# A fused top-k attention and feed-forward kernel: the first pair loaded in parts, and identity products ahead of it

## The chip, the cores and the metric

The kernel runs on one core of a Trainium2 chip. The time is device microseconds of one execution. The kernel before was run six times; the time quoted for it is the median, 874.3 us. One further execution was recorded by the hardware profiler, and every duration below comes from it.

## The reference

For 8 batches and 8 heads, with 576 positions and a head dimension of 64, each row of attention scores keeps its 32 largest entries. The softmax runs over those alone. The heads are laid side by side to rows of 512, and these go through a feed-forward with a squared ReLU.

```python
scores = scale * np.matmul(q, k.transpose(0, 1, 3, 2))
kth = np.partition(scores, -top_k, axis=-1)[..., -top_k:-top_k + 1]
mask = scores >= kth
scores = np.where(mask, scores, -1000000000.0)
...
attn = attn / (np.sum(attn, axis=-1, keepdims=True) + 1e-09)
return np.matmul(attn, v).astype(np.float32)
...
h = x @ w_in
r = np.maximum(h, 0.0)
g = r * r
return (g @ w_out).astype(np.float32)
```

The inputs are float32: q, k and v of 8 x 8 x 576 x 64, w_in of 512 x 2048, w_out of 2048 x 512. The output is 4608 x 512.

## The kernel before

**Tiles.** Two heads make a pair, and there are 32 pairs. The 576 query rows of a pair make four groups of 128 rows (gi 0 to 3) and a rest of 64 rows; the rests of two pairs make one more group (gi is Z). That gives 144 groups, each with 128 query rows of two heads on the partitions. The feed-forward works on chunks of up to 256 rows as soon as all heads of those rows are done.

**What one pair and one group go through.**

- `load_pair` loads q, k and v of a pair (tiles rq, rk, rv; two buffers each). q and k take three DMAs each (L469 twice, L472), v takes five (L479, L483). TensorE transposes q and k in blocks of 128 rows against a float32 identity (through the helper at L447): four blocks of q, four of k, and two short blocks of 64 rows. ScalarE copies the results from PSUM to the tile qk (L511 to L514). POOL converts v to bf16 (L515).
- `top_k` makes the scores of one group: eight float32 products into three PSUM banks (helper at L444). There is one such set of banks, so the next group's scores wait until the present ones are read. ScalarE copies them to s (L555). VectorE reads PSUM and s for pairwise maxima (L611, twice), which are merged once more (L621). POOL makes the matching minima from sums on the int32 patterns (L606). Then VectorE takes eight maxima at a time (L638), replaces them (L642), three times for each head, and takes the last eight over all 576 (L645), whose last one is the 32nd largest.
- ScalarE marks what is below it (w, L653). `attend` transposes the scores back with that mask added (L447, L444), ScalarE takes the exponential (p, L687), and `collect` multiplies with v and scales by the reciprocal of the sum (L714 to L742, the reciprocal on VectorE, L716).
- `feed` does the feed-forward of a chunk: products with win, ReLU (L768), square (L779 on VectorE for the last chunk, L782 on POOL), products with wo, copy (L802), store.
- `setup` makes the identities on POOL and loads and converts the sixteen weight parts (L891, L894). Their staging lies in two buffers.

PSUM has eight banks: three for the scores, two for `attend` together with one more (ps_q, which the merge shares), and two (the pool `psum`) for every transposition of q and k and every product of `collect` and `feed`.

**What sets the order.** Every operation is recorded in a plan with an engine, an assumed duration, a priority (the smaller the earlier), the tiles that it reads and writes, and the buffers that it takes. `schedule` plays this plan: each time an engine is free it starts the ready operation of the smallest priority whose buffers are free. The order so found on each engine is fixed and written out. On the chip each engine runs its list in order, and waits on semaphores for what the list needs. The assumed durations thus give the order; they don't give the time. A store or load on the SP list is assumed to hold SP for 0.6 per DMA, and to end 2.3 after that. `nbf` is the earliest assumed time of an operation, and `after` and `order` name operations that must come before. A load with `via="act"` is planned in SP's list, but issued at the start by ScalarE; k of the first pair is such a load.

The priorities of a group are built from its due time `tg = T0 + PER * n`, with n the number of the group, and constants at L320 to L340:

- ME and MQ set how early VectorE merges the maxima of a group (L611 and L621), in the same unit as PER.
- TW sets when its mask is made (L653).
- TA sets when `attend` is due; for the last NL groups, TL pulls it forward, by an amount that grows linearly to the end.
- WC sets the priority of the weight conversions, WN the earliest assumed time of their loads.
- LAGL delays the products of the feed-forward of the last batch.

Of the kernel before, what the change touches and what calls it, by code (L numbers as in the profile page):

```python
# [12 lines left out]
P = 128  # L13
# [278 lines left out]
def bass_top_k_attn__then__act_relu_squared_kernel(  # L292
# [27 lines left out]
    PER = 5.55  # L320
    T0 = 12.0
    LEAD = 40
    ME = 16.41
    MQ = 15.52
    MP = 18.0
    MA = 18.98
    SQ = 5.15
    TA = 7.2
    TW = -0.14
    TL = 8.0  # L330
    NL = 28.07
    WD = 3.33
    WC = 1.75
    WA = 1.13
    WN = 6
    NBO = 3.81
    LAG = 11.28
    STEP = 3.19
    LATE = 2.38
    LAGL = 11.07  # L340

    ident32 = sb("ident32", [P, P])
    ident_bf = sb("ident_bf", [P, P], BF16)
# [102 lines left out]
    def tr(o, i, ident, **kw):  # L446
        return pe.matmul(o, i, ident, is_transpose=True, skip_group_check=True, **kw)  # L447
# [3 lines left out]
    def build(full, weights, pl):  # L451
# [3 lines left out]
        def slot_sem(o):  # L455
            t = o.takes[0]
            return f"{t.pool.name}{t.slot}"

        def load_pair(b, hp, base):
            rq, rk, rv = tile("rq"), tile("rk"), tile("rv")  # L460


            def load(t, src, rest, queue=nc.sync):
                def fn():
                    r = at(t)
                    res = []
                    for h in range(2):
                        r0 = 64 if h and rest != (512, 512) else 0
                        res.append(queue.dma_start(r[:, 0:4, h, :], src[b, 2 * hp + h, r0:r0 + 512, :].rearrange(  # L469
                            "(tb p) d -> p tb d", p=P)))  # L470
                    x = src[b, 2 * hp, rest[0]:rest[0] + 64, :]
                    res.append(queue.dma_start(r[0:64, 4, :, :], bass.AP(  # L472
                        x.tensor, x.offset, [x.ap[0], [(S + rest[1] - rest[0]) * D, 2], x.ap[1]])))
# [12 lines left out]
            pl.op("sp", 2.3, base - 80, load(rq, q, (512, 512)), w=[rq], take=[rq], sem=slot_sem, ndma=3)  # L486
            via = "act" if not full and not state["pairs"] else None
            state["pairs"] += 1
            pl.op("sp", 2.3, base - 79.9, load(rk, k, REST, nc.scalar if via else nc.sync), w=[rk], take=[rk], sem=slot_sem,
                  ndma=3, via=via)  # L490
            pl.op("sp", 2.3, base - 70, loadv, w=[rv], take=[rv], sem=slot_sem, ndma=5)
            qk, vb = tile("qk"), tile("vb")
            tq, tk, tx = Tile(psum), Tile(psum), Tile(psum)
# [18 lines left out]
            pl.op("act", .6, base - 42.4, lambda: act.copy(at(qk)[:, 640:1152], bank(tk)), r=[tk], w=[qk])  # L512
            pl.op("act", .3, base - 42.3, lambda: act.copy(at(qk)[:, 512:640], bank(tx)[:, 0:128]), r=[tx], w=[qk])
            pl.op("act", .25, base - 42.2, lambda: act.copy(at(qk)[:, 1152:1216], bank(tx)[:, 64:128]), r=[tx], w=[qk])  # L514
# [311 lines left out]
        for b in range(NB):  # L826
            seq, stages = batch_order(b)
            pairs, held = {}, {}
            last = b == NB - 1
            for hp, gi in seq:  # L830
                tg = T0 + PER * state["n"]
                hps = (hp, hp if gi != Z else hp + 1)
                for x in hps:
                    if x not in pairs:
                        pairs[x] = load_pair(b, x, tg)
                st, wt = top_k(gi, [pairs[x][0] for x in hps], tg)
                tt = tg + PER + 2 - TA - TL * max(0, 1 - (NGRP - state["n"]) / NL)
# [12 lines left out]
                if left[i] == 0:  # L850
                    tm = T0 + PER * state["n"] + (NBO if not last else 8)
                    c = CHUNKS[i]
                    feed(c, xts[i], tm, (STEP if b < NB - 2 else 1.9) if not last else (1.5 if c is not CHUNKS[-1] else .5))
        return kths, rzs

    def setup(pl):
# [22 lines left out]
        for i in range(16):  # L879
# [121 lines left out]
```

## Time and profile before

| What | Value |
|---|---|
| Median of six runs | 874.3 us |
| The six runs | 875.54, 874.66, 868.26, 873.94, 869.92, 874.95 us |
| The profiled execution: its time | 868.97 us |
| The profiled execution: its span | 867.2 us |
| TensorE busy (matmul) | 803.4 us, 93% |
| VectorE busy | 822.4 us, 95% |
| ScalarE busy | 759.8 us, 88% |
| POOL busy | 788.0 us, 91% |
| Chain that ended last, by engine | DVE 64%, PE 16%, ACT 9% |
| First VectorE instruction starts | 12.55 us |
| Last selection on VectorE (L645) starts | 837.53 us |

The span runs from the first recorded event to the last one; the execution's own time is 1.8 us longer. In the profile PE is TensorE's matrix unit, PEld its loading of the stationary operand, DVE is VectorE, ACT is ScalarE, POOL is GpSimd, and SPq is the list from which SyncE issues DMAs. A line of a timeline has the start in us, the duration in us, the engine, the line of the kernel, the operation, the tiles written and read, the shapes, and how many instructions were merged; the bracket at its end gives the idle time ahead of it and who ended it. A line of a stretch has its bounds and length, and then for each engine the busy time and the number of instructions, the granted TensorE clock, the share of the DMA engines, and GB/s. A line of the waits has the waiting engine and line, who was waited for, the sum in us, how often, and the longest. In the slices, each digit is the busy share of a fortieth of the span, in tenths.

### The profile page before, as it was taken

How to read it: one execution, taken by the hardware profiler on the slowest of the kernel's cores; microseconds unless marked ns; L12 is line 12 of the kernel's file. 1: busy time of each engine (PE TensorE's matmuls, PEld its weight loads, DVE VectorE, ACT ScalarE, POOL GpSimd, SP SyncE). 2: the span in 40 equal slices, each digit the busy share in tenths (PEclk: the TensorE clock that was granted, in tenths of full speed). 3: DMA queues.
4: the chain of work that ended last, by engine and by line, in shares of the span. 5: the costliest groups of instructions: out<-in, count | busy, mean ns of one | idle time of the engine just before them, and what ended most of it. 6: DMA issues, size and time to landing. Idle time of an engine off the chain costs nothing.

```text
span 867.2 us, 22447 instructions
## 1 busy us (share of the span) xinstructions
PE 803.4 (93%) x7911; PEld 607.7 (70%) x7970; DVE 822.4 (95%) x3413; ACT 759.8 (88%) x1261; POOL 788.0 (91%) x826
## 2 busy tenths in 40 slices
PE   4577999989999999998999999999999999999996
PEld 3455777767687777766777677777777767677784
DVE  2989999999999999999999999999999999999971
ACT  4877998989898898989989899889999889898973
POOL 6989999999999998999999889998999987999971
PEclk9999999999999999999999999999999999999999
DMA  7982212130210223012131022202221021100000
GB/s 178 227 213 60 45 41 57 28 95 17 55 43 14 67 56 80 18 40 56 29 89 25 25 65 58 71 14 55 46 67 42 14 52 44 41 2 14 26 22 33
DMA packets 126969, 48.21 MB, mean 56 GB/s; under 512 B 119168, under 2 KB 119168, under 8 KB 126848
## 3 DMA queue, kind: packets, MB, share of 16 engines
q1 hardware_dynamic: 125648, 46.39, 21.4%
q8 instruction: 65, 1.06, 0.5%
q14 instruction: 56, 0.46, 0.2%
q10 hardware_dynamic: 1200, 0.30, 0.2%
HBM read 37.22 MB, written 9.44 MB: 54 GB/s over the span
## 4 chain that ended last, share of the span: by engine, by line
DVE 64%; PE 16%; ACT 9%; issue 5%; DMA 2%; POOL 2%; SPq 2%; DVEq 0%
DVE f L642 21%; DVE c L638 16%; DVE kth L645 13%; PE ps L444 12%; DVE f L621 5%; DVE ps L611 5%; DVE m L611 4%; PE ps L447 4%; ACT s L555 2%; ACT p L687 2%; ACT w L653 1%; DMA rk<-in_k_dram 1%; ACT g L768 1%; POOL f L606 1%; POOL t L606 1%
## 5 line engine op out<-in xcount | busy, mean ns | idle before, releaser
L642 DVE MATCH_REPLACE8 f<-c,f 128x104 f32<-128x104 f32 (+2 forms) x864 | 267.2, 315 | 0.0
L638 DVE MAX8 c<-f 128x8 f32<-128x104 f32 (+2 forms) x864 | 244.0, 319 | 0.0
L447 PE MATMUL ps<-ident,s 128*128 128x128 f32 x1296 | 221.8, 280 | 21.9 <-ACT p L687 14.1
L653 ACT ACTIVATE w<-s,kth 128x576 bf16<-128x576 f32 x288 | 222.8, 786 | 19.9 <-DVE kth L645 18.7
L444 PE MATMUL ps<-qk 64*128 64x64 f32 (+3 forms) x1280 | 211.0, 449 | 8.1 <-DVE m L611 6.7
L606 POOL TENSOR_TENSOR t<-s 128x576 int32<-128x576 int32 x144 | 202.4, 1411 | 12.7 <-ACT s L555 12.6
L645 DVE MAX8 kth<-f 128x8 f32<-128x576 f32 x288 | 207.5, 747 | 0.0
L606 POOL TENSOR_TENSOR f<-t,m 128x576 int32<-128x576 int32 x144 | 203.1, 1411 | 0.1
L555 ACT COPY s<-ps 128x1152 f32<-128x1152 f32 x144 | 161.4, 1121 | 31.6 <-PE ps L444 30.6
L444 PEld LDWEIGHTS ps<-qk 64*128 64x128 f32 (+1 forms) x1280 | 130.5, 178 | 83.4 <-issue 61.9
L447 PEld LDWEIGHTS ps<-ident,s 128*128 128x128 f32 x1296 | 143.4, 141 | 48.1 <-ACT p L687 22.9
L687 ACT ACTIVATE p<-ps 128x1152 bf16<-128x1152 f32 x144 | 163.3, 1134 | 8.8 <-PE ps L444 8.0
L444 PE MATMUL ps<-steep_bf,w 128*128 128x128 bf16 x1296 | 140.8, 219 | 0.0
L444 PE MATMUL ps<-wo,g 128*128 128x512 bf16 x517 | 127.9, 379 | 4.0 <-issue 1.1
L606 POOL TENSOR_TENSOR t<-m 128x288 int32<-128x288 int32 x144 | 114.8, 797 | 17.2 <-ACT m L619 13.7
L444 PE MATMUL ps<-xt,win 128*128 128x256 bf16 (+1 forms) x1152 | 126.6, 261 | 1.5 <-ACT qk L511 0.8
L606 POOL TENSOR_TENSOR f<-t,f 128x288 int32<-128x288 int32 x144 | 114.8, 797 | 0.0
L444 PEld LDWEIGHTS ps<-xt,win 128*128 128x128 bf16 x1152 | 97.9, 98 | 15.9 <-ACT g L768 1.2
L444 PEld LDWEIGHTS ps<-steep_bf,w 128*128 128x128 bf16 x1296 | 105.7, 100 | 4.1
L782 POOL TENSOR_TENSOR g<-g 128x512 bf16<-128x512 bf16 x92 | 95.5, 1040 | 12.9 <-ACT g L768 11.7
L768 ACT ACTIVATE g<-ps 128x512 bf16<-128x512 f32 x144 | 86.0, 606 | 10.2 <-PE ps L444 9.3
L444 PEld LDWEIGHTS ps<-wo,g 128*128 128x128 bf16 x576 | 51.3, 98 | 47.9 <-ACT xt L742 0.6
(60 smaller groups left out, 879.2 us busy)
## 6 DMA issues: line engine op xcount, KB each, us to landing
rq<-in_q_dram SPq DMA_DIRECT2D x64, 128.0 KB, 2.5
rv<-in_v_dram SPq DMA_DIRECT2D x64, 128.0 KB, 2.4
out_dram<-o SPq DMA_DIRECT2D x32, 256.0 KB, 2.1
rk<-in_k_dram SPq DMA_DIRECT2D x62, 128.0 KB, 2.6
g<-in_moe_w_in_dram SPq DMA_DIRECT2D x8, 512.0 KB, 4.5
g<-in_moe_w_out_dram SPq DMA_DIRECT2D x8, 512.0 KB, 4.8
rv<-in_v_dram SPq DMA_DIRECT2D x96, 16.0 KB, 2.2
rq<-in_q_dram SPq DMA_DIRECT2D x32, 32.0 KB, 2.8
```

The costliest lines, as they stand in the source:

```text
L444: return pe.matmul(o, l, r, start=start, stop=stop, skip_group_check=True)
L447: return pe.matmul(o, i, ident, is_transpose=True, skip_group_check=True, **kw)
L555: cp = [pl.op("act", 1.2, tg - LEAD + 1, lambda: act.copy(at(st)[:, :, :], two(banks(ss), SECOND, S)), r=[ss], w=[st])]
L606: return pl.op("gp", dur, prio, lambda: gp.tensor_tensor(o().bitcast(I32), x().bitcast(I32), y().bitcast(I32), op), **kw)
L611: return vec.tensor_tensor(o, two(banks(ss)[:, a:], SECOND + HALF, QUART), two(at(st)[:, 0, HALF + a:], HALF, QUART), ALU.max)
L638: lambda i=i, t=t, c0=c0, c1=c1: vec.max(eighth(t, i), at(f)[:, i, c0:c1]),
L642: lambda i=i, t=t, c0=c0, c1=c1: vec.match_replace(at(f)[:, i, c0:c1], eighth(t, i), at(f)[:, i, c0:c1], NEG), hold=[f])]
L645: ks.append(chain(kth, i, prev[i] + [low], .665, lambda i=i: vec.max(eighth(kth, i), at(f)[:, i, :]), hold=[f]))
L653: pl.op("act", .77, tw + .8 * i, lambda i=i: act.activation(at(wt)[:, i, :], at(st)[:, i, :], ACTF.Relu, bias=kth[:, i, n:n + 1], scale=-1.0),
L687: pl.op("act", 1.15, tt + 1, lambda: act.activation(at(pt)[:, :, :].rearrange("p k q -> p (k q)"), banks(e)[:, 0:2 * S], ACTF.Exp, scale=0 ...
L768: return act.activation(at(g)[:, 0:kf * nt], bank(hh)[:, 0:kf * nt], ACTF.Relu)
L782: pl.op("gp", .15 + w_ / 480, tf + lag + 1, lambda g=g: gp.tensor_tensor(at(g)[:, 0:w_], at(g)[:, 0:w_], at(g)[:, 0:w_], ALU.mult), u=[g])
```

## The change

Four things are changed.

- **The loads of the first pair.** k is loaded first in the plan, still issued by ScalarE. q comes in two tiles: its first 128 rows of both heads (two DMAs), and then the rest (three DMAs) into the second rq buffer. Other pairs are loaded as before.
- **The transpositions of the first pair.** The first block of q, then the four full blocks of k, then the short block of k are transposed. VectorE copies the four blocks of k from PSUM; ScalarE copies the block of q, and the short block of k twice (to both ends of k's part of qk). The first group's scores are planned next. The other blocks of q, their copy, and the conversion of v are recorded after the first group's selection, by `later`.
- **Identity products.** Thirty-six products of the bf16 identity with itself repeated four times (512 columns) are planned for TensorE at the lowest priority. Each takes one bank of the pool `psum`, may start once the identity is made, and has an earliest assumed time 0.22 after the one before it. Nothing reads their results. With WEND equal to WARM, the second list of times is empty.
- **Constants.** Ten constants are changed or new.

```diff
-    ME = 16.41
-    MQ = 15.52
+    ME = 20.33
+    MQ = 19.99
...
-    TW = -0.14
-    TL = 8.0
-    NL = 28.07
+    TW = -1.88
+    TL = 12.76
+    WARM = 8
+    WSTEP = 1.2
+    WEND = 8
+    NL = 36.74
...
-    WC = 1.75
+    WC = 2.52
...
-    LAGL = 11.07
+    LAGL = 12.15
...
+            pl.op("sp", 2.3, base - 82, start(nc.scalar, lambda: part(rk, k, 0, 0, 4), lambda: part(rk, k, 1, 0, 4),
+                                           lambda: rest(rk, k, REST[0], REST[1] - REST[0])),
+                  w=[rk], take=[rk], sem=slot_sem, ndma=3, via="act")
+            pl.op("sp", 2.3, base - 81, start(nc.sync, lambda: part(rq, q, 0, 0, 1), lambda: part(rq, q, 1, 0, 1)),
+                  w=[rq], take=[rq], sem=slot_sem, ndma=2)
+            pl.op("sp", 2.3, base - 79, start(
+                nc.sync, lambda: part(rq2, q, 0, 1, 3), lambda: part(rq2, q, 1, 1, 3), lambda: rest(rq2, q, 512, 0)),
+                w=[rq2], take=[rq2], sem=slot_sem, ndma=3)
...
+            o_x = pl.op("pe", .15, base - 45.2, flips(tx, rq, [0]), r=[rq], w=[tx], take=[tx, qk])
+            o_k = pl.op("pe", .5, base - 45.1, flips(tk, rk, [0, 1, 2, 3]), r=[rk], w=[tk], take=[tk], order=[o_x])
+            pl.op("pe", .2, base - 45, lambda: tr(bank(tx)[:, 128:192], at(rk)[0:64, 4, :, :].rearrange("p h d -> p (h d)"),
+                                                  ident32[0:64, 0:64]), r=[rk], w=[tx], order=[o_k])
+            pl.op("act", .3, base - 42.5, lambda: act.copy(at(qk)[:, 0:128], bank(tx)[:, 0:128]), r=[tx], w=[qk])
+            pl.op("dve", .6, base - 42.5, lambda: vec.tensor_copy(at(qk)[:, 640:1152], bank(tk)), r=[tk], w=[qk])
+            for i, c in enumerate((576, 1152)):
+                pl.op("act", .25, base - 42.4 + .1 * i, lambda c=c: act.copy(
+                    at(qk)[:, c:c + 64], bank(tx)[:, 128:192]), r=[tx], w=[qk])
+
+            def later():
+                pl.op("pe", .5, base - 44, flips(tq, rq2, [1, 2, 3, 4]), r=[rq2], w=[tq], take=[tq])
+                pl.op("act", .6, base - 42, lambda: act.copy(at(qk)[:, 128:576], bank(tq)[:, 0:448]), r=[tq], w=[qk])
+                pl.op("gp", .8, base + 5, lambda: gp.tensor_copy(at(vb)[:, :, 0:D], at(rv)[:, :, :]),
+                      r=[rv], w=[vb], take=[vb])
+
+            state["more"] = later
+            return qk, vb
...
                 st, wt = top_k(gi, [pairs[x][0] for x in hps], tg)
+                if state.get("more"):
+                    state.pop("more")()
...
+        times = [.22 * i for i in range(int(WARM / .22))]
+        times += [WARM + WSTEP * i for i in range(int((WEND - WARM) / WSTEP))]
+        for x in times:
+            t = Tile(psum)
+            pl.op("pe", .22, 1e5, lambda t=t: mm(bank(t), ident_bf[:, :], ident_bf[:, :].unsqueeze(1).broadcast_to(
+                [P, 4, P]), True), w=[t], take=[t], after=[i2], nbf=x)
```

More of the change, by code (lines that the diff above doesn't have):

```diff
@@ L457, in slot_sem, with load_first, part, rest @@
             return f"{t.pool.name}{t.slot}"
+        def load_first(b, hp, rq, rq2, rk, base):
+            def part(t, src, h, tb, n_):
+                r0 = 128 * tb + (64 if h and src is k else 0)
+                return at(t)[:, tb:tb + n_, h, :], src[b, 2 * hp + h, r0:r0 + 128 * n_, :].rearrange(
+                    "(tb p) d -> p tb d", p=P)
+            def rest(t, src, r0, d0):
+                x = src[b, 2 * hp, r0:r0 + 64, :]
+                return at(t)[0:64, 4, :, :], bass.AP(x.tensor, x.offset, [x.ap[0], [(S + d0) * D, 2], x.ap[1]])
+            def start(queue, *parts):
+                return lambda: [queue.dma_start(*x()) for x in parts]
+            pl.op("sp", 2.3, base - 82, start(nc.scalar, lambda: part(rk, k, 0, 0, 4), lambda: part(rk, k, 1, 0, 4),
[6 more added lines that the diff above has]
+                w=[rq2], take=[rq2], sem=slot_sem, ndma=3)
@@ new lines, in first_pair, with flips, fn @@
+        def first_pair(rq, rq2, rk, rv, qk, vb, base):
+            tk, tx, tq = Tile(psum), Tile(psum), Tile(psum)
+            def flips(o, src, tbs):
+                def fn():
+                    for i, tb in enumerate(tbs):
+                        n_ = 64 if tb == 4 else 128
+                        ins = tr(bank(o)[:, 128 * i:128 * i + n_], at(src)[0:n_, tb, :, :].rearrange("p h d -> p (h d)"),
+                                 ident32[0:n_, 0:n_])
+                    return ins
+                return fn
+            o_x = pl.op("pe", .15, base - 45.2, flips(tx, rq, [0]), r=[rq], w=[tx], take=[tx, qk])
[14 more added lines that the diff above has]
+            return qk, vb
@@ L459, in load_pair, with load @@
         def load_pair(b, hp, base):
             rq, rk, rv = tile("rq"), tile("rk"), tile("rv")
-            def load(t, src, rest, queue=nc.sync):
+            def load(t, src, rest):
                 def fn():
@@ L468, in fn @@
                         r0 = 64 if h and rest != (512, 512) else 0
-                        res.append(queue.dma_start(r[:, 0:4, h, :], src[b, 2 * hp + h, r0:r0 + 512, :].rearrange(
+                        res.append(nc.sync.dma_start(r[:, 0:4, h, :], src[b, 2 * hp + h, r0:r0 + 512, :].rearrange(
                             "(tb p) d -> p tb d", p=P)))
                     x = src[b, 2 * hp, rest[0]:rest[0] + 64, :]
-                    res.append(queue.dma_start(r[0:64, 4, :, :], bass.AP(
+                    res.append(nc.sync.dma_start(r[0:64, 4, :, :], bass.AP(
                         x.tensor, x.offset, [x.ap[0], [(S + rest[1] - rest[0]) * D, 2], x.ap[1]])))
@@ L484, in loadv @@
                 return res
-            pl.op("sp", 2.3, base - 80, load(rq, q, (512, 512)), w=[rq], take=[rq], sem=slot_sem, ndma=3)
-            via = "act" if not full and not state["pairs"] else None
+            via = not full and not state["pairs"]
             state["pairs"] += 1
-            pl.op("sp", 2.3, base - 79.9, load(rk, k, REST, nc.scalar if via else nc.sync), w=[rk], take=[rk], sem=slot_sem,
-                  ndma=3, via=via)
+            if via:
+                rq2 = tile("rq")
+                load_first(b, hp, rq, rq2, rk, base)
+            else:
+                pl.op("sp", 2.3, base - 80, load(rq, q, (512, 512)), w=[rq], take=[rq], sem=slot_sem, ndma=3)
+                pl.op("sp", 2.3, base - 79.9, load(rk, k, REST), w=[rk], take=[rk], sem=slot_sem, ndma=3)
             pl.op("sp", 2.3, base - 70, loadv, w=[rv], take=[rv], sem=slot_sem, ndma=5)
             qk, vb = tile("qk"), tile("vb")
+            if via:
+                return first_pair(rq, rq2, rk, rv, qk, vb, base)
             tq, tk, tx = Tile(psum), Tile(psum), Tile(psum)
```

## Prediction

> **What bounds the kernel now.** I read the busy shares first, then the slices, then who VectorE waited for, then the first 20 us instruction by instruction, and last the end.
>
> ```profile
> PE 803.4 (93%) x7911; PEld 607.7 (70%) x7970; DVE 822.4 (95%) x3413; ACT 759.8 (88%) x1261; POOL 788.0 (91%) x826
> ...
> PE   4577999989999999998999999999999999999996
> ...
> DVE  2989999999999999999999999999999999999971
> ```
>
> VectorE is busy 95%, and the slices say where the rest is: at both ends. Cut into stretches, VectorE is busy 50.0 of every 50 us from 100 to 750. So a saving counts if it starts VectorE earlier, fills its holes before 100 us, or shortens what follows its last selection. All of VectorE's waits over 3 us:
>
> ```profile
> DVE ps L611 <- ACT s L555: 15.3, 2, 12.5
> DVE rzall L716 <- ACT av L714: 7.7, 3, 4.4
> DVE g L779 <- ACT g L768: 6.3, 4, 4.9
> DVE ps L611 <- ACT p L687: 3.7, 4, 2.0
> ```
>
> The first line is the start: 12.5 us before the first score copy, and 2.72 before the second. The second and third are the end. The fourth belongs to the holes at 41.8, 50.0 and 74.3 (0.17, 2.04 and 1.15 us). The start as a timeline:
>
> ```profile
> 5.95 1.09 PE L447 MATMUL ps<-ident,rq 128*128 128x128 f32 x4 [5.95 <-DMA rq<-in_q_dram]
> ...
> 7.92 0.58 ACT L512 COPY qk<-ps 128x512 f32<-128x512 f32 x1 [0.27 <-PE ps L447]
> ...
> 8.85 2.50 PE L444 MATMUL ps<-qk 64*128 64x64 f32 x8 [0.56 <-ACT qk L514]
> ...
> 11.40 1.12 ACT L555 COPY s<-ps 128x1152 f32<-128x1152 f32 x1 [2.60 <-PE ps L444]
> ...
> 12.55 0.47 DVE L611 TENSOR_TENSOR ps<-ps,s 128x288 f32<-128x288 f32 x1 [12.55 <-ACT s L555]
> ...
> 13.43 2.50 PE L444 MATMUL ps<-qk 64*128 64x64 f32 x8 [2.08 <-DVE m L611]
> ...
> 18.45 1.35 PE L444 MATMUL ps<-qk 64*128 64x64 f32 x8 [0.48 <-DVE f L642]
> ```
>
> The same eight score products take 2.50 us twice, then 1.35: TensorE runs at half speed until about 17.0 (four transpositions fall from 1.09 to 0.66). The clock column shows only recorded changes and reads 1.00 there; later it shows what closes the clock. Stretches of 3.4 us, with PE's busy time as the first pair of numbers:
>
> ```profile
> 40.90:44.30 3.40, 1.38 (x14) 1.26 (x16) 3.23 (x17) 3.40 (x6) 3.16 (x5) 1.00 1.04 238
> 44.30:47.70 3.40, 3.40 (x29) 2.55 (x30) 3.40 (x14) 1.13 (x3) 3.40 (x4) 0.50 0.73 180
> ...
> 13.60:17.00 3.40, 3.40 (x14) 2.56 (x15) 0.77 (x3) 1.81 (x2) 3.27 (x4) 1.00 0.79 193
> ...
> 6.80:10.20 3.40, 2.84 (x13) 2.22 (x13) 0.00 (x0) 1.46 (x4) 0.83 (x1) 1.00 0.93 247
> ```
>
> A stretch with 1.38 us of work is followed by 3.4 us at 0.50; a fully busy one ends it. Counted in such steps back from 44.3, the first opening at 17.0 ended a fully busy step too, and the step 6.8 to 10.2, busy 84%, did not open it.
>
> **The change, part by part.** All terms are against the profiled execution, 868.97 us (span 867.2 and 1.8 around it).
>
> **(1) The identity products.** They need only the bf16 identity, which POOL ends at 2.00. 36 are made (8/.22). How many stand ahead of the first transposition follows from the code's own durations, which fix an order and not a time: the identity is ready at 1.4 there, the first block of q at 5.3, and (5.42 - 1.52)/.22 gives 18. TensorE runs in order, so on the chip all 18 run first, whenever the load lands. No row shows a 512-column product at half speed. At full speed 15 came in 3.40 us, 0.227 each; times 2.50/1.35 that is an estimate of 0.42. So 18 take 4.1 to 7.6 us. The clock opens at the end of the first fully busy step, 3.4 to 6.8 us after 2.05: at best 8 slow ones, end at 7.7; in the middle 12 slow and 6 fast, end at 8.5; at worst all slow, 9.6. I take 8.5. Today's transpositions start at 5.95, so the products, not the loads (rq's last landing 5.81, rk's 6.08), would be late next: +2.55.
>
> [...]
>
> **(2) First transpositions and copies.** Now k, five blocks, plus one block of q: at full speed 0.17 + 0.66 us, then a short one (0.2): 9.5. VectorE copies 512 columns from PSUM, which no row shows: its 288-column operations there take 0.45, which gives 0.45 to 0.83; ACT's copy of this tile takes 0.58, the nearest, so 0.6. It lies beside ACT's three copies, of which the two of 64 columns (0.23 each) come after the short transposition: both end near 9.95. One product can slip in (0.23). Score at 10.2, 1.35 long; copy 1.12 with 0.05 on either side; VectorE starts at 12.8 instead of 12.55: **+0.2** (from -0.8 in the best case of (1) to +1.3 in the worst).
>
> **(3) Second score.** It starts when VectorE has read the first one's PSUM, and today takes 2.50. At full speed it gains 1.15. But the gap ahead of it (11.35 to 13.43, 2.08) now holds q's other transpositions (0.66) and 7 products (1.6), by the same count: 2.3, or 0.2 over; with one PSUM bank free, each would wait for the one before (0.4 each, from the 379 ns that the page's costliest groups give as the mean of one 128x512 product): 3.5, or 1.4 over. I take 0.2: **-1.0** (-1.2 to +0.3). The rest of the 36 lie where TensorE has 7.5 us of holes between 20 and 40.
>
> **(4) Queues.** SP issues q's first block in two DMAs, then q's rest in three, ahead of v: two issues more, about 1 us later for v, the first weight and the second pair. k stays on ACT's queue. v is read by POOL at 7.49, for a product at 46: covered. But q's rest takes the second rq buffer, so the second pair's q, issued at 6.23 today, waits for the first transposition, near 8.6. Everything on SP behind it moves 2.4 us: its last k issue from 9.12 to 11.5, landing after 4.2 (the longest) at 15.7. Its transpositions run at 15.85 and 16.76 today: 0, with 1 us to spare.
>
> **(5) New constants.** ME and MQ raise the priority of VectorE's merge of the next scores by 4 us, TW delays the masks by 1.7, TL and NL pull the last attention forward, LAGL delays the last feed-forward by 1.1, WC delays the weight casts. Casts end by 72 and the first weight product is at 94.85: 0. No row shows an order that is not run. VectorE's holes after the second score and before 100 are 0.26 + 0.17 + 2.04 + 1.02 + 1.15 = 4.6; the largest follows a load that TensorE awaited 3.0 us and the half clock of 44.3 to 47.7 (scores 2.38, not 1.35). All could go, or as many could come (+4.6). The earlier merge speaks for less; I take a third: **-1.5**.
>
> The end: the last selection ends at 838.9, 28.3 before the end of the span.
>
> ```profile
> 837.53 1.41 DVE L645 MAX8 kth<-f 128x8 f32<-128x576 f32 x2
> ...
> 857.07 3.40 PE L444 MATMUL ps<-wo,g 128*128 128x512 bf16 x15
> ```
>
> The chain of that group alone, by its rows: mask .78, transpositions 1.65, exponential 1.13, product .49, copies and scaling 1.3, feed-forward 7.2, copy .58, store and end 6.1: 19.2. The other 9 are TensorE's backlog. A new order could save at most 9, or put one feed-forward (7.2) behind the chain; nothing says which, so I stay near zero: **-0.5**.
>
> Sum: 868.97 + 0.2 - 1.0 - 1.5 - 0.5 = **866.2**.
>
> **Against the median.** The six times lie in two clumps, 868.26 and 869.92, and 873.94 to 875.54; the profile is of the lower. My reading (not shown by one trace): TensorE's busy stretch 13.43 to 17.97 is 4.5 long, and contains a whole 3.4 us step in (4.5 - 3.4)/3.4, a third of the cases; two of six are in the lower clump. 18 products make a stretch of 7.6 us at half clock, which always contains one. So the upper clump should go, and I forecast 866.2 for the median: 0.9% under 874.3. Kept clumps would give 874.3 - 2.8 = 871.5.
>
> **Rivals.**
> - **Clumps stay** (0.14): the sum holds but the spread has another cause, such as the closings at 44.3 and 68.2, which remain: 871.5, within 0.5%.
> - **TensorE's backlog eats the gain** (0.10): from 823 to 860.5 it is hardly idle, so an earlier VectorE waits at the end for the same 803 us of work. For it: 97% busy from 100 on. Against it: its holes before 100 (32 us) shrink with the start. 869 to 874.
> - **The products don't open the clock** (0.04): end 9.6, transpositions .27 + 1.06, copy .6, score 2.5, copy 1.2: VectorE at 15.3, +2.7, so 872 to 877.
> - **All goes well** (0.14): best cases of (2), (3), all 4.6 of the holes, 2 of the end: 868.97 - 0.8 - 1.2 - 4.6 - 2 = 860.4.
> - **Slower: q's buffer** (0.08). If the first transposition is later than about 9.6 (1 us of spare in (4)), the second pair's k is late, TensorE stands before it in order, the score of the third group behind it, and SP's order passes the lateness to the next three pairs. Today a wait of 3.0 for such a load preceded a VectorE hole of 2.04; four of them with the +1.3 and half-clock scores (1.15) after each idle step: 4 x (2.04 + 1.15) + 1.3 = +14, lessened by 1.0: 882, above 878.7.
>
> **Numbers.** A forecast case 0.50. 0.5% is about what a measurement of this kernel tells from no change: 869.9 and 878.7. Faster 0.50 + 0.14 = 0.64; within: 0.14 + 0.10 + 0.04 = 0.28; slower 0.08. The range, 859.5 to 873.5, reaches from all going well to most of the clump and backlog cases; left out are the slower case, the clock case and about half of the backlog one, under 0.2.
>
> **What would show it.** (1) about 18 products from 2.1 on, the first transposition at 7.7 to 9.6 behind a product and not behind a DMA. (2) VectorE's first wait 11.7 to 13.8. (3) both first scores near 1.35; second wait under 2. (4) no wait for rk before 20. (5) VectorE's holes at 20 to 100 nearer 3 than 4.6; last selection to end near 28. If VectorE starts before 11.5, my count or price of products is wrong; if the end moves by more than 5 against the last selection, the constants did it.

## The result, and the profile after

The changed kernel takes 875.8 us (median of 21 runs, 873.8 to 877.8); the kernel before, by then in 48 runs, 873.4 us (868.3 to 877.0). The ratio is 1.0031, with an interval of [1.0019, 1.0042]. That is a small loss, where the forecast had a gain of 0.9%, and the time lies above the stated range (873.5). The profiled execution took 877.04 us with a span of 875.2, so 8.0 us more span than the profiled execution of before. Much of these 8 comes from which two executions were profiled: before's 868.97 lies at the low end of its 48 times, the new one at the upper end of its 21. The medians differ by 2.4. Each trace also records its granted TensorE clock; the mean is 0.994 in the profile of before and 0.986 in the new one.

In the changed kernel L673 is the old L611, L683 the old L621, L700, L704 and L707 are the old L638, L642 and L645, L447 the old L444, and L450 the old L447. VectorE's waits after, as a list with the sum in us, how often, and the longest:

```profile
DVE ps L673 <- ACT s L617: 11.5, 7, 3.1
DVE qk L502 <- PE ps L450: 9.8, 1, 9.8
...
DVE ps L673 <- ACT p L749: 5.2, 7, 1.6
```

The first long wait has become two: VectorE starts with the copy of k at 9.81, and then waits for the first scores. But it now waits for a copy of scores seven times, not twice. TensorE's first 28 us:

```profile
2.06 7.00 PE L447 MATMUL ps<-ident_bf 128*128 128x512 bf16 x18 [2.06 <-POOL ident_bf L924]
8.90 0.32 PE L450 MATMUL ps<-ident,rq 128*128 128x128 f32 x1
...
10.88 1.34 PE L447 MATMUL ps<-qk 64*128 64x64 f32 x8
...
12.85 3.09 PE L447 MATMUL ps<-ident_bf 128*128 128x512 bf16 x8
15.87 1.35 PE L447 MATMUL ps<-qk 64*128 64x64 f32 x8
17.14 0.84 PE L447 MATMUL ps<-ident_bf 128*128 128x512 bf16 x3
...
18.30 2.63 PE L447 MATMUL ps<-ident_bf 128*128 128x512 bf16 x6
20.99 0.66 PE L450 MATMUL ps<-ident,rk 128*128 128x128 f32 x4
...
22.60 1.35 PE L447 MATMUL ps<-qk 64*128 64x64 f32 x8 [0.69 <-ACT qk L576]
26.03 2.50 PE L447 MATMUL ps<-qk 64*128 64x64 f32 x8 [2.08 <-DVE m L673]
```

The scores are at full speed, as meant, until 26 (1.34 and 1.35 us for eight, then 2.50). But almost no line has a bracket with a wait: TensorE is busy nearly throughout, and much of that is identity products. Eighteen stand ahead of the first transposition, one ahead of the first score, eight ahead of the second, nine more ahead of the second pair's k at 20.99. VectorE's first three steps of a group's selection (L673, the old L611) come at 13.44, 18.42 and 25.15; before, they came at 12.55, 17.13 and 21.13. The second and third, after and then before:

```profile
18.42 0.47 DVE L673 TENSOR_TENSOR ps<-ps,s 128x288 f32<-128x288 f32 x1 [3.12 <-ACT s L617]
...
25.15 0.47 DVE L673 TENSOR_TENSOR ps<-ps,s 128x288 f32<-128x288 f32 x1 [1.19 <-ACT s L617]
```

```profile
17.13 0.47 DVE L611 TENSOR_TENSOR ps<-ps,s 128x288 f32<-128x288 f32 x1 [2.72 <-ACT s L555]
...
21.13 0.46 DVE L611 TENSOR_TENSOR ps<-ps,s 128x288 f32<-128x288 f32 x1
```

Stretches of 3.4 us show the clock (bounds, length, then busy time of PE, PEld, DVE, ACT, POOL, then the granted clock):

```profile
18.10:21.50 3.40, 3.04 (x14) 1.09 (x12) 3.08 (x15) 2.02 (x4) 3.10 (x4) 1.00 0.29 69
21.50:24.90 3.40, 1.75 (x12) 1.09 (x10) 2.46 (x8) 2.71 (x5) 1.61 (x2) 1.00 0.75 196
24.90:28.30 3.40, 2.27 (x8) 1.59 (x8) 3.15 (x16) 1.86 (x4) 3.10 (x4) 0.52 1.05 252
```

When the products run out, a stretch with 1.75 us of work follows, and the granted clock is recorded at half from 25.05 to 31.87. So it opens during the products, at 7.98, and doesn't stay open.

The end:

```profile
844.73 1.41 DVE L707 MAX8 kth<-f 128x8 f32<-128x576 f32 x2
```

The last selection ends at 846.14, 7.2 us later than before; what follows takes 29.1 instead of 28.3. Where the 7.2 come from can be read off VectorE's idle times. Summed up from the brackets of its timeline they are, in us (the last column is all the time from there to the end of the span):

| | to 20 us | 20 to 100 | 100 to last selection | from last selection to end |
|---|---|---|---|---|
| before | 15.3 | 5.0 | 0.8 | 28.3 |
| after | 15.9 | 7.7 | 3.4 | 29.1 |

That is 5.9 of idle time (0.6, 2.7 and 2.6) and 0.7 for the copy of k, which VectorE now does itself; the rest is in slightly longer instructions.

### The profile page after: what moved, and what is told of

Same layout as the page of the kernel before. It is cut to its first block, busy times and chain, and to the rows that moved or that the text cites. A ratio compares the mean times of both kernels' runs of the same rounds, so it can differ in the third digit from the quotient of the medians.

```text
span 875.2 us, 22504 instructions
## 1 busy us (share of the span) xinstructions
PE 819.1 (94%) x7948; PEld 613.5 (70%) x8006; DVE 823.9 (94%) x3414; ACT 761.0 (87%) x1261; POOL 789.3 (90%) x826
## 3 DMA queue, kind: packets, MB, share of 16 engines
q8 instruction: 65, 1.06, 0.5%
## 4 chain that ended last, share of the span: by engine, by line
DVE 58%; PE 25%; ACT 9%; issue 4%; POOL 2%; DMA 1%; SPq 0%; DVEq 0%; POOLq 0%
DVE f L704 19%; PE ps L447 18%; DVE c L700 15%; DVE kth L707 12%; PE ps L450 7%; DVE f L683 4%; DVE ps L673 4%; DVE m L673 4%; ACT p L749 3%; ACT s L617 2%; ACT w L715 1%; POOL t L668 1%; POOL f L668 1%; DMA g<-in_moe_w_out_dram 1%; DVE rzall L778 0%
## 5 line engine op out<-in xcount | busy, mean ns | idle before, releaser
L704 DVE MATCH_REPLACE8 f<-c,f 128x104 f32<-128x104 f32 (+2 forms) x864 | 267.2, 315 | 0.0
L700 DVE MAX8 c<-f 128x8 f32<-128x104 f32 (+2 forms) x864 | 245.8, 319 | 0.0
L450 PE MATMUL ps<-ident,s 128*128 128x128 f32 x1296 | 224.4, 283 | 22.7 <-ACT p L749 15.7
L668 POOL TENSOR_TENSOR t<-s 128x576 int32<-128x576 int32 x144 | 202.9, 1415 | 18.9 <-ACT s L617 18.6
L447 PE MATMUL ps<-qk 64*128 64x64 f32 (+3 forms) x1280 | 208.8, 445 | 7.0 <-DVE m L673 4.3
L707 DVE MAX8 kth<-f 128x8 f32<-128x576 f32 x288 | 206.7, 747 | 0.0
L447 PEld LDWEIGHTS ps<-qk 64*128 64x128 f32 (+1 forms) x1280 | 129.4, 177 | 80.6 <-issue 60.7
L450 PEld LDWEIGHTS ps<-ident,s 128*128 128x128 f32 x1296 | 145.2, 142 | 49.0 <-ACT p L749 21.7
L447 PE MATMUL ps<-steep_bf,w 128*128 128x128 bf16 x1296 | 141.2, 220 | 0.0
L447 PE MATMUL ps<-wo,g 128*128 128x512 bf16 x518 | 130.0, 381 | 4.2 <-issue 1.3
L447 PE MATMUL ps<-xt,win 128*128 128x256 bf16 (+1 forms) x1152 | 128.5, 262 | 2.7 <-ACT xt L804 0.9
L447 PEld LDWEIGHTS ps<-xt,win 128*128 128x128 bf16 x1152 | 97.5, 98 | 18.7 <-ACT g L830 2.3
L447 PEld LDWEIGHTS ps<-steep_bf,w 128*128 128x128 bf16 x1296 | 106.0, 100 | 4.4
L844 POOL TENSOR_TENSOR g<-g 128x512 bf16<-128x512 bf16 x92 | 95.8, 1044 | 11.9 <-ACT g L830 11.6
L447 PEld LDWEIGHTS ps<-wo,g 128*128 128x128 bf16 x576 | 52.2, 98 | 47.4 <-ACT xt L804 0.9
```

What stands on the lines that cost most here:

```text
L447: return pe.matmul(o, l, r, start=start, stop=stop, skip_group_check=True)
L668: return pl.op("gp", dur, prio, lambda: gp.tensor_tensor(o().bitcast(I32), x().bitcast(I32), y().bitcast(I32), op), **kw)
L700: lambda i=i, t=t, c0=c0, c1=c1: vec.max(eighth(t, i), at(f)[:, i, c0:c1]),
L704: lambda i=i, t=t, c0=c0, c1=c1: vec.match_replace(at(f)[:, i, c0:c1], eighth(t, i), at(f)[:, i, c0:c1], NEG), hold=[f])]
L707: ks.append(chain(kth, i, prev[i] + [low], .665, lambda i=i: vec.max(eighth(kth, i), at(f)[:, i, :]), hold=[f]))
L844: pl.op("gp", .15 + w_ / 480, tf + lag + 1, lambda g=g: gp.tensor_tensor(at(g)[:, 0:w_], at(g)[:, 0:w_], at(g)[:, 0:w_], ALU.mult), u=[g])
```

## The experiments

Each version was compared with the kernel before on the same chip. The median of before was between 871.1 and 872.9 us in the four sets, so ratios are compared, not times. Three theories (possible causes) were tried: **P**, the products' own time on TensorE; **C**, the constants; **O**, that any newly planned order, whatever is planned, moves the time. **Q**, the late loads of the second pair, and **W**, the half-clock steps, came beside them.

### The products made short, in the same order

```diff
+        for j, x in enumerate(times):
...
-                [P, 4, P]), True), ...
+                [P, 4, P]), True) if j < FIRST else mm(bank(t)[:, 0:64], ident_bf[:, :], ident_bf[:, 0:64], True), ...
```

FIRST stands for 0 or 18: with 0 all products are short (64 columns instead of 512), with 18 the later ones.

> The changed kernel with the same order of instructions on every engine, but each of the 36 identity products 64 columns wide instead of 512. Theory P (the products stand in TensorE's way: 7.0 us ahead of the first transposition, 3.1 ahead of the second score, 2.6 ahead of the second pair's k, in the changed kernel's timeline): first transposition between 5.5 and 6.5 instead of 8.9, VectorE's first selection step at 11.4 to 12.2 instead of 13.44 although the first scores run at half clock again (2.50), third group's step near 22 instead of 25.15; time 870 to 873. Theory C (the ten constants give the loss, by holes after 100 us and a longer end): the start is earlier, but the time stays 874.5 to 877. Theory Q (q of the first pair fills both buffers, so the second pair's loads are late): the second pair's q is issued at 6.5 to 7.5 instead of 9.25, time 872 to 874.

Measured: ratio 1.0032 [1.0015, 1.0048], 873.9 us. P had expected 870 to 873. TensorE's first lines:

```profile
2.06 2.64 PE L447 MATMUL ps<-ident_bf 128*128 128x64 bf16 x18 [2.06 <-POOL ident_bf L924]
4.70 0.47 PE L450 MATMUL ps<-ident,rq 128*128 128x128 f32 x1
...
7.24 2.50 PE L447 MATMUL ps<-qk 64*128 64x64 f32 x8
...
10.80 2.00 PE L447 MATMUL ps<-ident_bf 128*128 128x64 bf16 x8
```

A product an eighth as wide is not an eighth as long: 18 of them take 2.64, for 7.00 in the changed kernel, and the eight later ones 2.00, 0.25 each. The clock opened only at 28.5 (four transpositions take 1.11 at 27.30 and 0.61 at 29.03), and four scores took 2.50. VectorE's first step did come early (10.9), but the third at 24.0, and P's time was missed. Q's two numbers came (the second pair's q was issued at 7.11, and the time lies in its 872 to 874); what speaks against Q is the changed kernel's own trace, further down. The slow clock alone doesn't explain this time: the version without products, below, has the same order and its first four scores at 2.50 too, and is at 0.9999 with its third step at 21.5. What it lacks is the short products; by their rows 4.3 us of them stand between the first score and the second pair's k here. So this version speaks for P in kind, and its time was missed because a short product is not cheap (0.147 to 0.29 each).

> The changed kernel with the same order of instructions, the first 18 identity products at 512 columns and the 18 later ones at 64. Theory P: the first step of VectorE stays near 13.4, the second comes at 17.0 to 17.4 instead of 18.42 (second score right after VectorE has read the first), the third near 22 instead of 25.15, if the clock stays open; time 872 to 874.5. If the late products are what keeps the clock open, the second or third score goes back to 2.5 us and the gain is 1 us less. Theory C: 874.5 to 877.

Measured: 1.0018 [1.0002, 1.0034], 873.2 us; first three steps at 11.9, 15.6 and 21.6. The clock closed at 18.8 and was at half until 29.0 (scores of 2.08 at 18.30 and 2.50 at 22.46, then 1.35 at 30.24). P had expected 872 to 874.5, but the first step near 13.4; C 874.5 and more.

### Parts of the change alone, planned anew

Constants alone in the kernel before:

```diff
-    ME = 16.41
+    ME = 20.33
...
-    LAGL = 11.07
+    LAGL = 12.15
```

> The kernel before with the seven changed constants alone (no identity products, first pair loaded as before). Theory C: 875 to 877, with holes of VectorE after 100 us and an end longer than 28.5 after its last selection. Theory P: 872 to 874, as the kernel before.

Measured: 1.0055 [1.0037, 1.0074], 876.1 us, with an end of 31.4 after the last selection, as C had it.

The new first pair alone (the changed kernel with the old constants and WARM and WEND 0):

```diff
-    WARM = 8
+    WARM = 0
...
-    WEND = 8
+    WEND = 0
```

> The kernel before with the first pair's new loads, transpositions and copies alone (old constants, no identity products). Theory P: transposition of k at about 6.1 at half clock, VectorE's copy near 7.3, scores at 8.0 for 2.5 us, VectorE's first step at 11.5 to 12.0 instead of 12.55; time 871.5 to 873.5. Theory Q: the second pair's q waits little here (first transposition near 5.5), but q's and v's later issues shift it by 1 us; 872 to 875.

Measured: 1.0020 [1.0004, 1.0036], 873.6 us. That is just above P's 871.5 to 873.5 and within Q's 872 to 875, and VectorE's first step came at 10.9, earlier than expected.

Both without the products (new constants, WARM and WEND 0):

> The changed kernel without any identity product (WARM and WEND 0); the order is planned anew. Theory P: first transposition at 5 to 6, first scores at half clock, VectorE's first step 11.4 to 12.0, time 870 to 873. Theory C: 874.5 to 877.

Measured: 0.9984 [0.9969, 0.9999], 871.3 us; steps at 10.6, 14.0 and 19.9. This is what P expects, and C doesn't.

The products alone, added to the kernel before (their loop in `setup`, with WARM and WEND 8):

> The kernel before with the 36 identity products alone (old loads, old constants). The plan's first pair is ready near 4.1 and 5.9 there, so about 12 to 19 products stand first. Theory P: first transposition at 7 to 9 instead of 5.95, first scores at 1.35, VectorE's first step between 12.5 and 14, time 874 to 877. Theory C: 872 to 874.

Measured: 1.0031 [1.0014, 1.0049], 875.4 us. The first step is at 13.8, but the end takes 32.0 us, which nothing at the start explains.

The changed kernel with the old values of the seven constants:

> The changed kernel with the seven constants of the kernel before (identity products and the new first pair stay). Theory C: 872 to 873.5. Theory P: 875 to 877, with VectorE's first step near 13.4 as in the changed kernel.

Measured: 1.0058 [1.0036, 1.0081], 877.6 us. C gets no support as the main cause: with the old constants the changed kernel is slower, not faster.

The products and the new constants with the old loads:

> The kernel before with the identity products and the new constants, but with the old loads of the first pair. Theory P: as products alone, 874 to 877. Theory C: 875 to 877. Theory Q (the new loads give the loss): below 874.5; if it is not below the changed kernel's 875.8, Q is out as a main cause.

Measured: 1.0058 [1.0034, 1.0083], 877.2 us. It is not below the changed kernel, so Q gets no support as a main cause. The changed kernel's own trace speaks against Q more directly: the second pair's transpositions, at 17.82 and 20.99, follow products without a wait for a load.

### One product every 1.2 us of the plan

```diff
-    WARM = 8
+    WARM = 0
...
-    WEND = 8
+    WEND = 80
```

> The changed kernel without the dense row of 36 products, but with one identity product every 1.2 us of the plan from 0 to 80. Theory W (half-clock steps between 15 and 80 us cost VectorE its holes there): the clock closes less often than in the five to six steps seen, holes from 20 to 100 us fall from 7 to about 3, time 867 to 870. Theory P: some 66 products in a free bank cost 0.2 to 0.45 us each where TensorE has 30 us of holes, but some stand ahead of scores: 871 to 875.

Measured: 1.0039 [1.0021, 1.0057], 875.2 us. Up to 100 us the clock closed twice only (at 18.6 and 52.8; its mean from 20 to 100 is 0.97, for 0.89 in the changed kernel), and the holes from 20 to 100 fell to 5.3, not to 3. The end took 32.8 us. W gets no support: a version with little time at half clock is among the slow ones. It also has products ahead of its early scores and a new order, so it doesn't price the clock by itself.

### The order kept, products taken out

The versions planned anew mix the products' time with a new order. Here, as with the short products, the planned order of the changed kernel is kept on every engine, and products are dropped from TensorE's list afterwards; waits that went through a dropped product's PSUM bank go to its user before that. KEEP stands for the number kept, 0, 8, 18 or 6.

```diff
     span = main.schedule()
+    drop = [o for o in main.order["pe"] if o.prio == 1e5][KEEP:]
+    gone = {o.takes[0]: o.takes[0].prev for o in drop}
...
+    main.order["pe"] = [o for o in main.order["pe"] if o not in drop]
+    main.ops = [o for o in main.ops if o not in drop]
```

> The changed kernel's planned order on every engine, with all 36 identity products taken out of TensorE's list after the planning. Without any product but planned anew it was 871.3, and with short products in this order 873.9. Theory P (the products' own time, of which a short one still costs 0.15 to 0.29 us, is the loss): VectorE's third step near 20 as in the version planned anew, 870 to 872. Theory O (the order that was planned around the products is the loss, not their time): 873 to 876, although the start is as early.

Measured: 0.9999 [0.9983, 1.0014], 871.7 us. P holds: the order that was planned around the products is not what costs, their time is, 0.0032 between this version and the changed kernel.

```profile
3.75 0.47 PE L450 MATMUL ps<-ident,rq 128*128 128x128 f32 x1 [3.75 <-DMA rq<-in_q_dram]
4.95 1.41 PE L450 MATMUL ps<-ident,rk 128*128 128x128 f32 x5 [0.73 <-DMA rk<-in_k_dram]
6.95 2.50 PE L447 MATMUL ps<-qk 64*128 64x64 f32 x8 [0.59 <-ACT qk L504]
```

These lines of TensorE's timeline also show what the new loads are worth by themselves: q's block is there at 3.75 and k at 4.95 in this execution (k at 5.75 in that of the version with six products, below); before, TensorE started at 5.95. VectorE's first step is at 10.7, 1.9 earlier than before, and its idle time to 20 us falls from 15.3 to 12.7. Yet the ratio is 1. In the two profiles more than these 2.6 is lost again: 1.3 as holes from 20 to 100 (6.3 for 5.0), 0.6 as later holes (1.5 for 0.8), 0.7 as the copy of k, and 1.4 at the end (29.7 for 28.3). The profile of before is one of its fastest executions, so their sum of 4.0 says where time is lost, not how much in the median.

> The changed kernel's planned order with only the first 8 identity products kept (8 x 0.427 us at half clock: 2.06 to 5.5, about when k lands). Theory P: products cost next to nothing here, VectorE's first step 10 to 11, time 870 to 872. If opening the clock is worth something, 1 us below the version with none; it opens in time only if a whole 3.4 us step lies in 2.06 to about 6.6, about one case in three, so the medians differ by less than 1 us. Theory O: 873 to 876.

Measured: 0.9975 [0.9959, 0.9992], 870.1 us. This version beats both kernels.

```profile
2.06 3.59 PE L447 MATMUL ps<-ident_bf 128*128 128x512 bf16 x8 [2.06 <-POOL ident_bf L924]
5.45 0.42 PE L450 MATMUL ps<-ident,rq 128*128 128x128 f32 x1
...
7.70 1.32 PE L447 MATMUL ps<-qk 64*128 64x64 f32 x8 [0.67 <-ACT qk L504]
...
11.10 1.35 PE L447 MATMUL ps<-qk 64*128 64x64 f32 x8 [1.40 <-DVE m L673]
```

Eight products end at 5.45, half a microsecond after k's landing in the version with none. The clock opened at 6.7 in this execution, so that the first scores run at full speed (1.32 and 1.35, for 2.50 in the version with none), 3.2 us earlier than in the changed kernel. VectorE's steps come at 10.2, 13.7 and 19.3; its idle times are 11.1, 6.9 and 1.5, and the end takes 28.7.

> The changed kernel's planned order with the first 18 identity products kept and the 18 later ones taken out (with none it was 871.7, ratio 0.9999; with the first 8, 870.1, 0.9975; with all 36, 1.0031). If the ten products between k's landing near 5 and the first transposition at 7.5 to 9 cost what they take: VectorE's first step 11.9 to 13.4, ratio 1.000 to 1.002 (2 to 4 us above the version with 8). If the 18 later ones are the loss: 0.998 or below.

Measured: 1.0005 [0.9990, 1.0019], 872.6 us, the first step at 13.0. This is what was expected if the ten products cost what they take. Its third step:

```profile
22.11 0.45 DVE L673 TENSOR_TENSOR ps<-ps,s 128x288 f32<-128x288 f32 x1
```

> The changed kernel's planned order with the first 6 products kept: 2.06 to 4.6, before k lands at 4.9. They wait for nothing and nothing waits for them. Theory P: within 1 us of the version with 8 (0.9975). If what counts in that version is that the clock opens ahead of the first scores, 6 products open it less often, and the ratio lies between 0.9975 and that with none, 0.9999.

Measured: 0.9990 [0.9971, 1.0008], 871.1 us. It lies between none and 8, but its interval holds both: whether opening the clock is worth anything beyond not being late stays open.

### Controls: a new order alone

```diff
-    NBO = 3.81
+    NBO = 3.86
```

This is the first control; the second changes LATE from 2.38 to 2.36 instead.

> The kernel before with a constant without bearing on the start nudged (NBO 3.81 to 3.86): the first 400 of some 1750 rows of TensorE's list stay the same, behind them the order differs. It measures what a new order alone does. Theory O: 2 to 5 us away from the kernel before, mostly slower, by a longer end after the last selection (above 29). Theory P: within 1.5 us of it.

Measured: 1.0065 [1.0039, 1.0091], 877.6 us. A nudge without purpose costs the kernel before twice what the change costs. Its profiled execution, 873.6 us, was the fastest of its seven, and its end of 29.0 us is not the long one that O had expected. In its profile VectorE's first four steps come within 0.3 us of those of before. Then it has holes that before doesn't have; three of its timeline's lines, with the idle time in the bracket:

```profile
33.36 0.47 DVE L611 TENSOR_TENSOR ps<-ps,s 128x288 f32<-128x288 f32 x1 [1.75 <-ACT p L687]
...
795.44 0.47 DVE L611 TENSOR_TENSOR ps<-ps,s 128x288 f32<-128x288 f32 x1 [0.81 <-ACT s L555]
...
828.21 0.47 DVE L611 TENSOR_TENSOR ps<-ps,s 128x288 f32<-128x288 f32 x1 [1.43 <-ACT s L555]
```

> A second control: the kernel before with the constant LATE 2.38 changed to 2.36; TensorE's list is the same for its first 1012 of some 1750 rows. Theory O (any new order costs the kernel before some us): slower by 1 to 5 us, less than the first control (1.0065) as less of the order is new. If the first control was a single bad draw: within 1 us of the kernel before.

Measured: 1.0035 [1.0015, 1.0056], 875.7 us.

The third control is the version with eight products with the same nudge of NBO:

> A third control: the version with 8 products with NBO 3.81 changed to 3.86; the first 413 rows of TensorE's list stay the same. Theory O: the chosen orders of both kernels are good draws, so this is slower than 0.9975 by 0.002 to 0.006. If orders scatter evenly, it may as well be faster.

Measured: 1.0007 [0.9991, 1.0023], 873.1 us: slower by 0.0032 than without the nudge. So all three controls are slower than the kernel that they nudge, by 0.0032 to 0.0065. Of the ten versions that were planned anew, seven parts and three controls, eight are slower than the kernel before, this one is level with it, and one is faster. Four of the six slower parts carry products as well, so it is the controls that speak for O: a new order moves the time, here three times out of three upwards. That the orders of both kernels were unusually good draws fits this, but three nudges don't show it. It follows that 0.003 between two versions that were planned anew decides little, and that what is said above of C, Q and W is support or its lack, and no proof.

## Why the prediction was wrong

The forecast was 8.1 us below the median of before; the result is 2.4 above. Of the 8.1, the sum of the terms made 2.8, and the step from the median down to the profiled execution 5.3. Both failed: the sum in (3) and (5), the step as a whole.

With the order kept, the ratios are: no products 0.9999, six 0.9990, eight 0.9975, eighteen 1.0005, eighteen and 18 short ones 1.0018, all 36 1.0031. Each has an interval of about ±0.0015, so a difference of two has about ±0.002. By them the ten products between k's landing and the first transposition cost 0.0030 (2.6 us), and the 18 later ones 0.0026 (2.3 us). The loads, the copies and the new order together, without products, give nothing that can be measured (0.9999). So the loss against before is the time of the products after the eighth; why the earlier start alone gained nothing is argued below, and not shown.

**The products, (1): right.** There are 18 ahead, by the count from the code's durations, 0.427 us each at half clock (from 3.15 to 7.85 their weight loads start so far apart), and the first transposition comes at 8.90, where I had 8.5. The clock opened at 7.98, within the bounds given. What (1) missed is how early the loads can be: I kept rk's landing at 6.08, as before, and in the version without products, in the same order, k is there by 4.95. So the products don't cost the 2.55 us against today's start alone; they also take the whole gain of the new loads at the start.

**First transpositions, (2): right in kind, small in size.** VectorE's first step came at 13.44, for 12.8. The copy of k took 0.69 for 0.6, and the product that could slip in did, at 0.39 for 0.23; it is in the bounds given.

**Second score, (3): this step failed, in two places.** "I take 0.2" for the gap: it took the far bound. With eight products in it the gap was 3.65 us (12.22 to 15.87) instead of 2.08: 1.6 over, where the far bound had 1.4. The first six run in one PSUM bank, as the plan still holds the other, and each waits for the one before:

```profile
13.29 0.10 PEld L447 LDWEIGHTS ps<-ident_bf 128*128 128x128 bf16 x1 [0.35 <-PE ps L447]
13.74 0.10 PEld L447 LDWEIGHTS ps<-ident_bf 128*128 128x128 bf16 x1 [0.35 <-PE ps L447]
14.19 0.10 PEld L447 LDWEIGHTS ps<-ident_bf 128*128 128x128 bf16 x1 [0.35 <-PE ps L447]
```

These weight loads of the changed kernel stand 0.45 apart at full clock, twice the 0.227 that I had; only the last products, in turn in both banks, start 0.22 apart (15.10, 15.32 and 15.55). VectorE's second step came 1.3 us later than before, where I had 0.8 earlier (0.2 and -1.0).

The other place is the sentence "The rest of the 36 lie where TensorE has 7.5 us of holes between 20 and 40". They don't: nine of them stand between 17.14 and 20.93, ahead of the second pair's k and with it of the third score. I had counted the products up to the second score and put the others at nothing without looking for the work that stands behind them. The third step fell from 1.3 us behind to 4.0 behind. Taking the 18 later products out (same order) takes the third step from 25.1 to 22.1, and 0.0026 off the time.

**Queues, (4): right.** The second pair's q was issued at 9.25 and the last part of its k at 12.07, for 8.6 and 11.5; nothing waited for them. The slower rival, q's buffer, did not come about.

**Constants and order, (5): the sign failed.** I took -1.5 from the holes and -0.5 from the end. The holes grew from 5.0 to 7.7 us and from 0.8 to 3.4, and the end from 28.3 to 29.1. (My 4.6 for the holes of before had left out one of 0.37 at 80.5.) The products are not the whole of it: without them, in the same order, the holes are 6.3 and 1.5 and the end 29.7, all longer than in the profile of before. For the holes I had given both signs the same bound, and then took the favourable side: "The earlier merge speaks for less". The controls suggest what belongs in that place: three orders that were merely new cost these kernels 0.32 to 0.65%. How much of the holes and of the end is due to each constant can't be told by versions that are planned anew, since each draws a new order; that stays open.

**The median: failed.** I read six times as two clumps, and took the 5 us between the profiled execution and the median off the forecast. With 48 times there is no gap: 27 lie between 873 and 875, 13 below 872, and some in each microsecond between. The products did narrow the spread (4.0 us, for 8.7), but not towards its lower end. But the clock does go with the spread: of the 119 executions of the kernel before that were timed beside the experiments, the 25 with a mean granted clock of 0.98 took 873.1 to 874.2 us, and of the 48 with 0.99 or more 42 took less than 871.2. The profiled one, with 0.994, belongs with the latter. The changed kernel's executions had 0.984 to 0.990. Which openings and closings make the difference can't be seen, as one trace of before was kept, and the clock doesn't rank the versions: the fastest, with eight products, had 0.982 to 0.986. The rivals that kept the spread or lost the gain at the end gave 869 to 874; none had a loss from the products' place in the order. The measured time does lie in the 872 to 877 of the rival in which the products don't open the clock, but by luck: they opened it.

## What to carry to other kernels

Filler work on TensorE's list isn't free because it has the lowest priority: the planner places it by assumed times, and on the chip what stood behind it waited (the first transposition of the changed kernel came at 8.90, behind 18 products; without products, in the same order, it came at 3.75), so count each piece by what stands behind it, and make the last one end about when the first loads land (here eight products, not 36). A start that is earlier by two microseconds can be lost again further on, as in the version without products; measure the scatter of a new order with a nudge that means nothing before crediting a change with less than that. Take a forecast for the median from the spread of many runs, not from one profiled execution at its edge.

## What the runs showed of the hardware

- Products of 512 columns that use one PSUM bank in turn, each waiting for the one before, start 0.45 us apart at full clock (changed kernel, 12.85 to 15.10); with two banks they start 0.427 apart at half clock (3.15 to 7.85) and 0.226 at full (8.22 to 8.67). Products of 64 columns, in the version with all products short and at half clock: six in a row, in the place where the changed kernel's stand 0.45 apart, take 1.73 us (from 16.43), 0.29 each; the 18 at the start, with two banks, take 2.64, 0.147 each on the mean, which is again 0.29 from one to the next of the same bank. From this I read that for these short ones the wait for the bank, not the columns, set the pace.
- Up to 850 us, half clock is recorded from 44.33 to 47.74 and from 68.22 to 71.63 before, and from 25.05 to 31.87, 45.52 to 48.94, 59.18 to 62.59, 72.83 to 76.25 and 325.42 to 328.83 in the changed kernel: 6.83 us the first of the changed kernel, 3.41 each of the others. TensorE was not idle in the 3.4 us ahead of three of them: it had 1.38 and 0.83 us of work before (ending at 44.3 and 68.2) and 1.75 in the changed kernel (shown above). With 2.27 us of work from 24.90 to 28.30, at half clock, the changed kernel's clock stayed at half until 31.87.
- In the version without products, in the kept order, the clock opened near 27.8 (four transpositions take 1.06 us at 25.68 and 0.61 at 28.06). TensorE was busy all of the 3.40 us from 24.10 to 27.50, most of it with transpositions (2.85 us of them from 24.77 to 27.84). From 17.30 to 20.70 it had 2.50 us of scores, and the scores at 22.34 still took 2.50.
- In (1) I had let the clock open at the end of a wholly busy stretch of 3.4 us. In the version with six products it was open by 5.75 (five transpositions take 0.83 us there, 1.41 at 4.95 in the version with none), and TensorE had been idle for 0.73 us just ahead of that.
- k's first load of 128 KB took 3.4 us from issue to landing before and 2.6 in the changed kernel, though it was issued at the same time (0.74 and 0.75) on the same queue. What differs beside it is q on the other queue, first in two loads of 32 KB, where it had two of 128 KB. That this is the cause was not tried by itself.
